# Block 3's output projection as seven quarter-block products, with the steps of blocks 3 to 5 in a new order

## The chip, the core and the metric

The kernel runs on one core of a Trainium2 chip (trn2). The metric is the device time of one execution in microseconds (us). Beside the times of several executions there is one profiled execution, from which all rows shown here come. Engines are named as the profile names them: PE is TensorE, PEld its weight loads, DVE VectorE, ACT ScalarE, POOL GpSimd, SP SyncE, which issues most DMAs.

## What is computed

The inputs q, k, v and alpha have the shape (4, 8, 768, 48): batch B, heads H, positions S, head width D. The first part is a gated linear attention, the second a bilinear feed-forward layer on its 3072 tokens of width 384:

```python
state = np.zeros((B, H, D, D))
for t in range(S):
    state = alpha[:, :, t, :, None] * state + np.einsum('bhd,bhe->bhde', k[:, :, t], v[:, :, t])
    y[:, :, t] = np.einsum('bhd,bhde->bhe', q[:, :, t], state)
x = y.transpose(0, 2, 1, 3).reshape(B * S, H * D)
out = ((x @ w_a) * (x @ w_b)) @ w_out      # 384 -> 1536 -> 384
```

## The kernel before, in words

The work is cut into six blocks (`chunks`, 0 to 5) of 512 tokens: a third of the sequence for two of the four batches. Blocks 4 and 5 are the last third. Each block goes through the attention of its tokens, the two input projections `x @ w_a` and `x @ w_b` in twelve slices f of 128 columns of the hidden width 1536, their product, and the output projection.

The order is written out by hand. `PROGRAM` (L17 on) is a list of steps `block: name arguments; ...`, and the loop at the end of the kernel issues one after the other. Each engine runs its own instructions strictly in that order; between engines, an instruction starts when its inputs are there and when the last readers of what it overwrites are through. PSUM is one tile of eight banks, and the steps name the bank that they use (a step of two banks names the first). The steps that matter here, by engine:

- PE: `a f * i` and `b f * i` (`ff`, L881) are the input projections of slice f into bank i, three matmuls of 512 columns. `o m half i` (`ff_o`, L903) is half of the output projection of 128 tokens, six matmuls of 384 columns. `P n i` and `P+ n i` (`block_mm`, L989) are the products of the other way to project, twelve matmuls of 192 columns each; `P+` adds to what its bank holds. The attention's steps are `K` (L752, state update from keys and values), `D u h i` (L797, scores, two banks), `SB`, `SA` and `Y` (L826, outputs, two banks). u is the batch of the block, h a half of the heads.
- ACT: `as f` (L887) copies an `a` slice out of PSUM into one of three `as_` tiles; `Mc` (L810) copies scores; `vs ... S` copies swapped values; `Tr ... S` copies turned keys (L918); `ot m S` and `z ... S` copy results into staging tiles `ot` (L918).
- DVE: `pr f` (L895) multiplies the two slices into `prod`, of which there are two buffers; `mk` and `mq` (L636) scale keys and queries; `M` (L806) and `Mm` (L814) apply the mask; `k` (L782, L783) updates the state; `X` copies the attention's output to `xT` (ACT L862, DVE L864); `TW n` and `S n` (L960, L971, L974) make the sums that the quarter-block products need; `ot m V` (L920) and `z ... V` (L1001) put results into staging tiles, the latter with an addition.
- SP: `T u` turns keys and queries by a transposing DMA (L705), `dl` loads decays (`bl`, L647), `st` (L936) and `zs` (L1007) store staging tiles.

The quarter-block way splits a block's `prod` (hidden width in two halves kk, tokens in two halves u) and `w_out` (hidden width in two halves, output width in two halves) into quarters and forms the four result quarters c11, c12, c21, c22 from seven products instead of eight:

- Four sums of weights (`TW 1` to `TW 4`), made once, and four sums of `prod` for each block (`S 1` to `S 4`; `S 3` in place of a quarter of `prod`).
- Products 1 and 2 give c11. Products 1 and 6 together are u2; u2 with 5 and 3 is c12; u2 with 7 and 5 is c22; u2 with 7 and 4 is c21. So 1, 6, 7 and 4 follow on each other in one bank, 5 and 3 in another.
- `z p1`, `z u2` and `z p5` copy partial results into staging tiles, `z c11`, `z c12` and `z c22` add one to a product, `z c21` copies.

Before, blocks 4 and 5 go this way and blocks 0 to 3 go through `ff_o`. The fourteen products of blocks 4 and 5 stand one behind the other at the end. A product's result has two groups g of 128 tokens, side by side in one bank. Staging tiles share four buffers. The sums of weights and of `prod` lie in tiles that loads and logarithms of the attention used (`late`, and `la`, of which there is one).

Of the kernel before, what the change touches and what calls it, by code (L numbers as in the profile page):

```python
# [17 lines left out]
0: cm 0; c1; cz 0 b P; ci; ld a 0b Y; c1a; ld a 0a Y; ln 0b; cu; cz 1 b P; fill 7 0; cu2 V; cz 0 q V; cus; ld k 0b Y; ld k 0a Y; B 0b 2; ld q 0b Y  # L18
0: ln 0a; B 0a 0; ld v 0 P; ld q 0a Y; ld a 1 P; cs 0 m P; E 0b i; mk 0b V; ld k 1 P; ld q 1 P; cm 1; W b 0 256; cz 0 v P; E 0b b; mq 0b V; ld v 1 P; W a 256 768; dk 0 2
0: C 0 1 3; E 0a i; mk 0a V; cz 1 q P; E 0a b; mq 0a V; v 0 S; Ce 0 1 V; fill 2 0; W a 0 256; de 0; W b 256 512; C 0 0 1; Ce 0 0 V; D 0 1 2; K 0 0 0; vs 0 0 S; W b 512 768  # L20
0: cs 1 m P
# [78 lines left out]
1: pr 2 0; a 10 0 4; as 10 0; a 7 0 5; M 1 0; a 1 0 6; Mm 1 1 V; b 4 0 7; pr 4 0; b 1 0 1; a 5 0 4; as 1 0; pr 1 0  # L100
# [9 lines left out]
1: as 6 0; a 0 0 0; b 0 0 7; pr 6 0; a 11 0 4; X 1 S; a 2 1 5; b 3 0 2; as 0 0; pr 0 0; as 11 0; a 3 0 3; as 3 0; a 8 0 4; b 9 0 0; b 2 1 1; a 6 1 3; pr 11 0  # L110
1: as 2 1; a 9 0 5; as 9 0; pr 3 0; o 2 0 2
# [252 lines left out]
def kernel(  # L364
# [768 lines left out]
```

## Time and profile before

| what | value |
|---|---|
| times of three runs | 190.29, 189.83, 189.74 us |
| median | 189.83 us |
| profiled execution, own time | 189.66 us |
| its span, first to last instruction | 187.9 us |
| instructions in the span | 6287 |
| granted TensorE clock | full in all slices |

A row of grouped instructions gives the line, the engine, the operation, what it writes and reads with its shapes, the count, then busy time in us and the mean duration of one in ns, and behind the second bar the time that the engine sat idle before them and what released it. A row of the timeline begins with the start in us from the span's start and the time to the end of the group; brackets hold the idle time before it. Matmuls overlap in the pipeline, so their spacing is read from starts and not from durations. A row for a stretch gives its length and then, for PE, PEld, DVE, ACT and POOL, the busy us and the count, then the granted clock, the share of the DMA engines and GB/s.

### The profile page before, as it was taken

The page shows a single profiled execution, that of the slowest core. Times are in us where ns is not written, and L with a number is a line of the kernel's source. Part 1 is how long each engine was busy: PE and PEld are TensorE (multiplying, and loading weights), DVE is VectorE, ACT ScalarE, POOL GpSimd, SP SyncE. Part 2 cuts the span into 40 slices and gives each one's busy share as a digit, 9 for nine tenths or more (in the row PEclk, how much of TensorE's full clock was granted, in tenths as well). Part 3 has the DMA queues.
Part 4 walks back from the last instruction along what each step waited for, and adds up shares of the span by engine and source line. Part 5 has one row for each costly group of instructions (what it writes and reads, how often), then busy time and mean ns, then how long its engine had stood idle before and what let it go on. Part 6 is the DMA issues. An engine that isn't in the chain of part 4 may idle for free.

```text
span 187.9 us, 6287 instructions
## 1 busy us (share of the span) xinstructions
PE 180.7 (96%) x2658; PEld 118.0 (63%) x2673; DVE 149.1 (79%) x267; ACT 119.2 (63%) x225; POOL 51.7 (28%) x74
## 2 busy tenths in 40 slices
PE   7979999999999999999999999999999999999992
PEld 3868885566788876645456645555556444448992
DVE  2587988889979799997898999997487988865641
ACT  4467685678984888796898768942567244443230
POOL 8999573995080510007100006000000000000000
PEclk9999999999999999999999999999999999999999
DMA  5999999999998999999999296989322000000233
GB/s 146 254 224 196 265 236 253 233 249 264 243 223 130 160 236 285 278 254 149 186 245 260 48 161 123 85 115 183 59 85 84 9 0 0 0 0 3 85 130 126
DMA packets 65774, 29.43 MB, mean 157 GB/s; under 512 B 55777, under 2 KB 64113, under 8 KB 65745
## 3 DMA queue, kind: packets, MB, share of 16 engines
q1 hardware_dynamic: 46976, 16.34, 40.9%
q0 software_dynamic: 18624, 12.58, 39.4%
q8 instruction: 21, 0.34, 0.7%
q10 hardware_dynamic: 144, 0.10, 0.2%
q14 instruction: 9, 0.07, 0.1%
HBM read 25.98 MB, written 4.74 MB: 164 GB/s over the span
## 4 chain that ended last, share of the span: by engine, by line
PE 86%; ACT 6%; DMA 3%; issue 2%; POOL 1%; DVE 0%; POOLq 0%
PE psum L881 47%; PE psum L903 16%; PE psum L989 7%; PE psum L826 5%; DMA v_t<-in_v_dram 3%; PE psum L797 3%; ACT vx L918 2%; PE psum L696 2%; PE psum L591 1%; ACT la L514 1%; PE psum L752 1%; PE psum L765 1%; PE psum L658 1%; PE psum L549 1%; PE psum L550 1%
## 5 line engine op out<-in xcount | busy, mean ns | idle before, releaser
L881 PE MATMUL psum<-xT,wa_t 128*128 128x512 bf16 (+1 forms) x264 | 56.5, 336 | 0.5 <-issue 0.2
L881 PE MATMUL psum<-xT,wb_t 128*128 128x512 bf16 (+1 forms) x262 | 56.0, 335 | 0.6 <-issue 0.3
L881 PEld LDWEIGHTS <-wa_t 128*128 128x128 bf16 x270 | 25.8, 98 | 19.9 <-issue 0.5
L881 PEld LDWEIGHTS <-wb_t 128*128 128x128 bf16 x270 | 25.6, 98 | 19.5 <-issue 0.3
L903 PE MATMUL psum<-wo_t,prod 128*128 128x384 bf16 x192 | 34.7, 326 | 0.0
L903 PEld LDWEIGHTS <-prod 128*128 128x128 bf16 x192 | 17.9, 98 | 11.8
L610 POOL TENSOR_TENSOR q_t<-q_t,ra 128x384 f32<-128x384 f32 x6 | 6.1, 1009 | 53.9 <-ACT ra L603 30.9
L918 ACT ACTIVATE ot<-psum 128x384 f32<-128x384 f32 (+1 forms) x20 | 9.7, 485 | 12.1 <-PE psum L989 8.0
L918 ACT ACTIVATE vx<-v_t 32x384 bf16<-32x384 bf16 x26 | 13.5, 521 | 0.5
L810 ACT ACTIVATE m<-psum 128x768 bf16<-128x768 f32 x14 | 11.0, 810 | 3.9 <-PE psum L797 3.9
L636 DVE TENSOR_TENSOR QKp<-q_t,beta 128x768 bf16<-128x768 f32 x10 | 9.5, 954 | 2.8 <-POOL q_t L610 1.7
L514 ACT ACTIVATE la<-a_t 128x1536 f32<-128x1536 f32 (+2 forms) x9 | 9.5, 1055 | 2.9 <-DMA a_t<-in_alpha_dram 2.9
L806 DVE TENSOR_TENSOR m<-psum,mask 128x768 bf16<-128x768 f32 x10 | 9.5, 953 | 0.8 <-PE psum L797 0.6
L636 DVE TENSOR_TENSOR QKp<-k_t,invb 128x768 bf16<-128x768 f32 x10 | 9.5, 954 | 0.3
L826 PE MATMUL psum<-m,vx 64*64 64x128 bf16 (+1 forms) x576 | 8.7, 205 | 0.0
L507 POOL DMA_DIRECT2D v_t<-in_v_dram x8 | 8.5, 1064 | 0.0
L989 PEld LDWEIGHTS <-prod 128*128 128x128 bf16 x96 | 8.0, 98 | 0.2
L1001 DVE TENSOR_TENSOR ot<-psum,ot 128x384 f32<-128x384 f32 x6 | 3.3, 557 | 5.9 <-PE psum L989 5.6
L826 PEld LDWEIGHTS <-vx 64*64 64x64 bf16 x576 | 7.6, 108 | 0.2
L826 PE MATMUL psum<-kqT,Sm 64*64 64x128 bf16 x144 | 7.3, 220 | 0.4 <-DVE Sm L779 0.4
L814 DVE TENSOR_TENSOR m<-m,mask 128x768 bf16<-128x768 bf16 x14 | 7.5, 551 | 0.0
L625 ACT ACTIVATE beta<-psum 128x384 f32<-128x384 f32 x10 | 4.8, 495 | 3.5 <-PE psum L596 3.4
(292 smaller groups left out, 341.2 us busy)
## 6 DMA issues: line engine op xcount, KB each, us to landing
out_dram<-ot SPq DMA_DIRECT2D x23, 192.0 KB, 2.1
q_t<-in_q_dram SPq DMA_DIRECT2D x3, 768.0 KB
k_t<-in_k_dram SPq DMA_DIRECT2D x3, 768.0 KB
a_t<-in_alpha_dram POOLq DMA_DIRECT2D x2, 768.0 KB, 12.1
v_t<-in_v_dram POOLq DMA_DIRECT2D x4, 384.0 KB, 7.5
a_t<-in_alpha_dram SPq DMA_DIRECT2D x2, 768.0 KB
a_t<-in_alpha_dram POOLq DMA_DIRECT2D x3, 384.0 KB, 8.2
k_t<-in_k_dram POOLq DMA_DIRECT2D x3, 384.0 KB, 7.1
```

The source lines that it names most:

```text
L507: eng.dma_start(out=t[:, us, hs].rearrange("p b h r d -> p (b h) (r d)"), in_=src[ch.b0 + us.start:ch.b0 + us.stop, hs, ch.s * 2 * C:(ch.s ...
L514: nc.scalar.activation(out=ch.la[:, us, hs].rearrange("p b h r d -> p (b h r d)"), in_=ch.a[:, us, hs].rearrange("p b h r d -> p (b h r d) ...
L610: eng.tensor_mul(x, x, by)
L636: eng.tensor_mul(QKp[ch.c % 2][:, u, j, :, hs, :D], src[:, u, hs].rearrange("p h r d -> p r h d"), f)
L806: nc.vector.tensor_mul(m, x, maskn())
L810: nc.scalar.activation(out=m, in_=x, func=AF.Copy)
L814: eng.tensor_mul(m, m, maskn())
L826: nc.tensor.matmul(o, lhsT=lhsT, rhs=rhs, start=(g, c) not in begun, stop=False, skip_group_check=True)
L881: nc.tensor.matmul(p, lhsT=(wa_t, wb_t)[w][:, kk, f * 128:(f + 1) * 128], rhs=ch.xT[:, kk, us, :], start=(kk == 0), stop=(kk == KT - 1))
L903: nc.tensor.matmul(op, lhsT=ch.prod[:, f, at:at + C], rhs=wo_t[:, f, :], start=(f == 0), stop=(f == NFF - 1))
L918: nc.scalar.activation(out=o_, in_=i_, func=AF.Copy)
L989: nc.tensor.matmul(o[:, g], lhsT=A[:, f, g * C:(g + 1) * C], rhs=W[:, f], start=(not more and g == 0 and f == 0), stop=(f == LH - 1), skip ...
```

## The change

The matmuls and vector instructions of blocks 0 to 2, and all steps up to block 4's last score step, stay as they are (some long lines of `PROGRAM` are only broken in two). From there on:

- Block 3 is projected by the seven products in place of `o`: four `S`, seven products, seven `z`, and four `zs` for four `st`.
- The steps of blocks 3, 4 and 5 stand in another order and partly in other banks. The products of blocks 3 and 4 now stand between input projections of the next blocks. Block 5's products stand partly between block 4's.
- Block 5's products 1, 6, 7 and 4 use two banks, one for each group g (`Q`, `Q+`: `apart=True`), and the halves of `z c21` are issued in the other order: ACT takes half 1, DVE half 0.
- Staging tiles share six buffers. The tiles for the sums are taken one at a time, when their first sum is made.

The list of steps after, from the point of difference on (the list before stands in the kernel):

```diff
+4: D 1 0 2; Mc 1 0; Y 0
+2: st 3 Y
+5: T 0
+3: b 0 * 4; a 10 * 5
+5: K * 0 2
+4: Mm 1 0 V
+3: as 10 *
+4: SA 1; Y 1; X 1 S
+3: b 10 * 3
+4: X 0 V
+3: pr 0 *; b 7 * 5
+4: a 3 * 7
+5: v 1 V
+4: a 8 * 6; a 6 * 4
+5: vs 1 0 S; T 1; dl
+3: pr 7 *
+4: as 8 *; as 3 *; b 8 * 5; b 3 * 1
+3: pr 10 *
+2: st 0 Y
+4: a 0 * 0
+5: Tr 0 V
+4: as 6 *
+4: pr 8 *; b 0 * 3; pr 3 *
+5: k * 0 V; D 0 0 4; Tr 1 S; D 1 0 6; D 1 1 1
+4: as 0 *; pr 0 *
+5: M 1 0; Mc 0 0
+4: a 9 * 0; b 6 * 5; pr 6 *
+5: Mc 1 1
+4: as 9 *
+5: SB 1 3; vs 1 1 S; D 0 1 1; M 0 1; SB 0 6; Mm 1 1 V; Mm 0 0 V
+4: a 4 * 0; a 11 * 5; as 11 *; TW 1 V; a 7 * 1; as 7 *; b 11 * 2
+5: vs 0 0 V
+4: pr 11 *; b 7 * 5
+3: S 1 V
+5: SA 0
+4: pr 7 *
+5: SA 1; vs 0 1 S; Y 1; Y 0
+3: P 2 1
+5: X 0 V
+4: b 5 * 2
+5: X 1 V
+4: TW 2 V; a 5 * 5
+3: P 1 6
+4: TW 3 V; b 9 * 4; pr 9 *; TW 4 V; a 10 * 3
+3: z p1 1 S
+4: b 2 * 7; as 10 *
+3: z c11 2 V
+4: a 2 * 4
+5: a 4 * 3
+4: as 5 *; pr 5 *
+5: a 0 * 1
+3: S 2 V
+4: as 2 *; pr 2 *; b 10 * 2
+3: S 3 V
+4: pr 10 *; a 1 * 4
+3: P+ 6 6
+4: as 1 *
+3: P 5 5
+5: a 1 * 2
+3: S 4 V
+4: b 4 * 4
+3: z p5 5 S
+4: as 4 *
+5: b 4 * 7
+3: zs c11 Y; P+ 3 5
+5: as 4 *
+3: z u2 6 S; z c12 3 V; P+ 7 6; z c22 7 V
+4: b 1 * 0
+5: a 7 * 3; a 10 * 5
+4: pr 1 *
+5: b 0 * 0; as 0 *
+4: pr 4 *
+3: P+ 4 6
+5: pr 4 *; a 8 * 1; as 8 *; pr 0 *; b 1 * 4; b 7 * 7; b 8 * 0; pr 8 *
+3: zs c22 Y
+5: b 9 * 1
+3: zs c12 Y
+5: as 7 *
+4: P 2 3
+3: z c21 4 S
+5: a 6 * 0; as 1 *; pr 1 *; as 10 *
+4: S 1 V; S 2 V; P 1 6
+5: b 10 * 2; a 5 * 4
+4: z p1 1 S
+5: pr 7 *; as 6 *
+4: P+ 6 6; z c11 2 V
+5: b 6 * 7; a 2 * 0
+4: S 3 V
+5: pr 10 *; pr 6 *
+5: a 9 * 5; b 2 * 7; a 11 * 2; as 2 *; as 9 *; pr 2 *
+4: z u2 6 S
+5: a 3 * 0; as 3 *; b 3 * 3; pr 3 *; b 5 * 5
+4: P 5 0
+5: pr 9 *; b 11 * 3; as 5 *; pr 5 *
+4: P+ 7 6
+5: as 11 *; Q 1 1
+4: z p5 5 S
+5: pr 11 *
+3: zs c21 Y
+5: P 2 7; S 1 V; S 2 V
+4: z c22 7 V; P+ 3 0; z c12 3 V; zs c11 Y; zs c22 Y
+5: S 3 V
+4: P+ 4 6
+5: z p1 1 S
+4: z c21 4 S
+5: S 4 V; Q+ 6 1; z c11 2 V; P 5 0; z u2 6 S
+4: zs c12 Y
+5: Q+ 7 1
+4: zs c21 Y
+5: z p5 5 S; P+ 3 0; z c22 7 V; Q+ 4 1; z c12 3 V; zs c11 Y; zs c22 Y; z c21 4 S 1; zs c12 Y; z c21 4 V 0; zs c21 S 1; zs c21 Y 0
```

The functions:

```diff
@@ -920,12 +960,12 @@
             eng.tensor_copy(o_, i_)
 
     def ff_out(ch, m, eng):
-        ch.ot[m] = wk.tile([128, d_model], F32, name="ot", bufs=4)
+        ch.ot[m] = wk.tile([128, d_model], F32, name="ot", bufs=6)
         evict(ch.ot[m], ch.pf["o", m], eng)
 
     def ff_outc(ch, m, h, eng):
         if m not in ch.ot:
-            ch.ot[m] = wk.tile([128, d_model], F32, name="ot", bufs=4)
+            ch.ot[m] = wk.tile([128, d_model], F32, name="ot", bufs=6)
         evict(ch.ot[m][:, part(h)], ch.pf["oc", m, h], eng)
 
     def rows_of(ch, m):
@@ -953,9 +993,10 @@
         return wo_t[:, kk * LH:(kk + 1) * LH, nn * HM:(nn + 1) * HM]
 
     def mix_w(n, eng):
-        if n == 1:
-            x, y = (late(t)[:, :2 * LH * HM].rearrange("p (w f e) -> p w f e", w=2, f=LH) for t in "ak")
-            mix.update({1: x[:, 0], 2: x[:, 1], 3: y[:, 0], 4: y[:, 1]})
+        at = (n - 1) // 2
+        if 2 * at + 1 not in mix:
+            x = late("ak"[at])[:, :2 * LH * HM].rearrange("p (w f e) -> p w f e", w=2, f=LH)
+            mix.update({2 * at + 1: x[:, 0], 2 * at + 2: x[:, 1]})
         a, b = {1: (quarter(0, 1), quarter(0, 0)), 2: (quarter(1, 1), mix.get(1)), 3: (quarter(1, 1), quarter(0, 1)), 4: (quarter(1, 0), mix.get(2))}[n]
         eng.tensor_sub(mix[n], a, b)
 
@@ -964,8 +1005,10 @@
         p11, p12, p21, p22 = (P[:, kk * LH:(kk + 1) * LH, u * NT // 2:(u + 1) * NT // 2] for u in range(2) for kk in range(2))
         if n == 1:
             x = late("q").rearrange("p (w f e) -> p w f e", w=2, f=LH)
-            y = wk.tile([C, 2, H, 2, D], F32, name="la", bufs=1).rearrange("p b h r d -> p (b h r d)").bitcast(BF16)
-            ch.S = {1: x[:, 0], 2: x[:, 1], 3: p21, 4: y[:, :LH * NT // 2].rearrange("p (f e) -> p f e", f=LH)}
+            ch.S = {1: x[:, 0], 2: x[:, 1], 3: p21}
+        if n == 4:
+            x = wk.tile([C, 2, H, 2, D], F32, name="la", bufs=1).rearrange("p b h r d -> p (b h r d)").bitcast(BF16)
+            ch.S[4] = x[:, :LH * NT // 2].rearrange("p (f e) -> p f e", f=LH)
         S = ch.S
         if n == 1:
             eng.tensor_add(S[1], p21, p22)
@@ -973,7 +1016,7 @@
             a, b = {2: (S[1], p11), 3: (p11, p21), 4: (p12, S[2])}[n]
             eng.tensor_sub(S[n], a, b)
 
-    def block_mm(ch, n, i, more):
+    def block_mm(ch, n, i, more, apart=False):
         P = ch.prod
         pure = {1: (0, 0), 2: (1, 0), 4: (1, 1)}
         if n in pure:
@@ -982,17 +1025,17 @@
         else:
             A = ch.S[{3: 4, 5: 1, 6: 2, 7: 3}[n]]
         W = {1: quarter(0, 0), 2: quarter(1, 0), 3: quarter(1, 1), 4: mix.get(4), 5: mix.get(1), 6: mix.get(2), 7: mix.get(3)}[n]
-        o = bank(i)[:, :2 * HM].rearrange("p (g e) -> p g e", g=2)
+        o = wide(i)[:, :, :HM] if apart else bank(i)[:, :2 * HM].rearrange("p (g e) -> p g e", g=2)
         ch.pf["z", n] = o
         for g in range(2):
             for f in range(LH):
-                nc.tensor.matmul(o[:, g], lhsT=A[:, f, g * C:(g + 1) * C], rhs=W[:, f], start=(not more and g == 0 and f == 0), stop=(f == LH - 1), skip_group_check=True)
+                nc.tensor.matmul(o[:, g], lhsT=A[:, f, g * C:(g + 1) * C], rhs=W[:, f], start=(not more and (apart or g == 0) and f == 0), stop=(f == LH - 1), skip_group_check=True)
 
     def block_out(ch, what, n, eng, half=None):
         hs = slice(0, 2) if half is None else slice(int(half), int(half) + 1)
         x = ch.pf["z", n][:, hs]
         if what not in ch.ot:
-            ch.ot[what] = wk.tile([128, d_model], F32, name="ot", bufs=4).rearrange("p (g e) -> p g e", g=2)
+            ch.ot[what] = wk.tile([128, d_model], F32, name="ot", bufs=6).rearrange("p (g e) -> p g e", g=2)
         o_ = ch.ot[what][:, hs]
         by = {"c11": "p1", "c12": "u2", "c22": "p5"}.get(what)
         if by is None:
@@ -1088,6 +1131,8 @@
         "S": lambda x, n, e: mix_p(x, int(n), ENG[e]),
         "P": lambda x, n, i: block_mm(x, int(n), i, False),
         "P+": lambda x, n, i: block_mm(x, int(n), i, True),
+        "Q": lambda x, n, i: block_mm(x, int(n), i, False, True),
+        "Q+": lambda x, n, i: block_mm(x, int(n), i, True, True),
         "z": lambda x, what, n, e, h=None: block_out(x, what, int(n), ENG[e], h),
         "zs": lambda x, what, e, h=None: block_store(x, what, ENG[e], h),
         "oc": lambda x, m, h, f, i: ff_oc(x, int(m), int(h), int(f), i),
```

More of the change, by code (lines that the diff above doesn't have):

```diff
@@ L17 @@
 PROGRAM = """
[L18 to L21, printed above, removed]
+0: cm 0; c1; cz 0 b P; ci; ld a 0b Y; c1a; ld a 0a Y; ln 0b; cu; cz 1 b P; fill 7 0; cu2 V
+0: cz 0 q V; cus; ld k 0b Y; ld k 0a Y; B 0b 2; ld q 0b Y; ln 0a; B 0a 0; ld v 0 P; ld q 0a Y; ld a 1 P; cs 0 m P
+0: E 0b i; mk 0b V; ld k 1 P; ld q 1 P; cm 1; W b 0 256; cz 0 v P; E 0b b; mq 0b V; ld v 1 P; W a 256 768; dk 0 2
+0: C 0 1 3; E 0a i; mk 0a V; cz 1 q P; E 0a b; mq 0a V; v 0 S; Ce 0 1 V; fill 2 0; W a 0 256; de 0; W b 256 512
+0: C 0 0 1; Ce 0 0 V; D 0 1 2; K 0 0 0; vs 0 0 S; W b 512 768; cs 1 m P
 1: ld a 0 P
```

93 lines of the change are left out of this document (11 added, 82 removed).

## The prediction

> **What bounds the kernel now.** I read the page first: the busy shares, the forty slices, the chain that ended last.
>
> ```profile
> PE 180.7 (96%) x2658; PEld 118.0 (63%) x2673; DVE 149.1 (79%) x267; ACT 119.2 (63%) x225; POOL 51.7 (28%) x74
> PE   7979999999999999999999999999999999999992
> PEclk9999999999999999999999999999999999999999
> PE 86%; ACT 6%; DMA 3%; issue 2%; POOL 1%; DVE 0%; POOLq 0%
> ```
>
> TensorE is busy in every slice and at full clock, and 86% of the chain is its work. The change touches only the stretch from about 124 us on, so the busy time by stretch and the chain's end come next.
>
> ```profile
> 124.44:145.25 20.81, 20.49 (x391) 12.08 (x389) 15.12 (x27) 11.03 (x19) 0.00 (x0) 1.00 0.53 93
> 145.25:170.45 25.20, 24.93 (x116) 11.40 (x118) 20.80 (x30) 10.60 (x18) 0.00 (x0) 1.00 0.02 8
> 170.45:184.31 13.86, 13.86 (x169) 13.79 (x167) 7.46 (x11) 3.59 (x8) 0.00 (x0) 1.00 0.23 78
> ```
>
> The columns after the length are PE, PEld, DVE and ACT busy. PE fills 59.28 of 59.87 us. VectorE has 16.5 us to spare, but it is the second engine (20.80 of 25.20 us in the middle stretch). So what leaves PE leaves the time, provided VectorE and ScalarE still hand over in time; and what follows PE's last instruction counts in full.
>
> **The seven products.** PE in order of time:
>
> ```profile
> 124.44 1.47 PE L881 MATMUL psum<-xT,wb_t 128*128 128x512 bf16 x5
> 125.75 0.81 PE L881 MATMUL psum<-xT,wa_t 128*128 128x512 bf16 x3
> 126.49 0.62 PE L752 MATMUL psum<-v_t,QKp 64*64 64x48 bf16 x28
> 132.03 3.09 PE L903 MATMUL psum<-wo_t,prod 128*128 128x384 bf16 x18
> 134.95 0.81 PE L881 MATMUL psum<-xT,wa_t 128*128 128x512 bf16 x3
> 135.60 0.81 PE L881 MATMUL psum<-xT,wb_t 128*128 128x512 bf16 x3
> 170.45 2.14 PE L989 MATMUL psum<-wo_t,prod 128*128 128x192 bf16 x24
> 183.32 1.15 PE L989 MATMUL psum<-k_t,prod 128*128 128x192 bf16 x12
> 170.61 13.87 PE psum L989 x168
> ```
>
> Durations overlap; starts give the spacing. Eighteen matmuls of 384 columns take 134.95 − 132.03 = 2.92 us, 162 ns each. Thirteen products of twelve 192-column matmuls lie between 170.45 and 183.32: 0.99 us a product, 82.5 ns a matmul. A 512-column step of three takes 0.65 us. Block 3 loses 48 matmuls of 384 columns (48 x 162 = 7.79 us) and gains 7 x 12 of 192 (84 x 82.5 = 6.93 us): **0.86 us less PE**. Nothing else on PE changes in number; the rest is order. A change of shape costs nothing visible (the rows at 134.95 and 135.60 follow on without a gap), so I put 0 for products that now stand singly, at most 0.05 us in all.
>
> A rule of the Trainium skill speaks against this step: "TensorE: Matmul & The Clock Gate", section "Back-to-back issue gap", gives pairs of weight load and matmul a sustained spacing of about 81 ns at 128 columns and 131 ns at 512. By it block 3 would cost at least 84 x 81 = 6.8 us against at most 48 x 131 = 6.3 us, an estimate of 0.5 us lost instead of 0.86 won. The rows disagree: 162 ns at 384 columns.
>
> **What the products add elsewhere.** Grouped by line and shape:
>
> ```profile
> L974 DVE TENSOR_TENSOR la<-prod,q_t 128x1536 bf16<-128x1536 bf16 x2 | 1.9, 950 | 0.0
> L1001 DVE TENSOR_TENSOR ot<-psum,ot 128x384 f32<-128x384 f32 x6 | 3.3, 557 | 5.9 <-PE psum L989 5.6 <-issue 0.3
> L920 DVE COPY ot<-psum 128x384 f32<-128x384 f32 x3 | 1.7, 556 | 0.7 <-PE psum L903 0.7
> L918 ACT ACTIVATE ot<-psum 128x384 f32<-128x384 f32 x9 | 4.4, 491 | 8.0 <-PE psum L989 5.6 <-DVE ot L1001 2.5
> 150.30 0.72 DVE L895 TENSOR_TENSOR prod<-as__3226,psum 128x512 bf16<-128x512 bf16 x1
> 150.58 0.60 ACT L887 ACTIVATE as__3236<-psum 128x512 bf16<-128x512 f32 x1 [0.70 <-PE psum L881]
> ```
>
> VectorE gets four sums (4 x 0.95) and three output adds (3 x 0.56) and loses three copies (3 x 0.56): +3.8 us. ScalarE gets four copies and loses one: +1.5 us. SP still issues four stores for block 3; POOL gets nothing. VectorE then has about 47 of 59 us, so by totals all of it lies beside PE, and only local waits can cost. I laid the new order out by hand with these rows, each step behind its own queue, its inputs, the last reader of its bank and tile. The places that matter:
>
> ```profile
> 125.12 0.95 DVE L636 TENSOR_TENSOR QKp<-k_t,invb 128x768 bf16<-128x768 f32 x1
> 125.99 0.55 DVE L814 TENSOR_TENSOR m<-m,mask 128x768 bf16<-128x768 bf16 x1
> 127.08 0.93 DVE L636 TENSOR_TENSOR QKp<-q_t,beta 128x768 bf16<-128x768 f32 x1
> 123.86 6.12 SPq L705 DMA_TRANSPOSE kqT<-QKp  x2
> 130.08 1.57 SPq L647 DMA_DIRECT2D bl<-row  x2
> 132.55 1.06 ACT L918 ACTIVATE kp<-kqT 128x1024 bf16<-128x1024 bf16 x1
> 133.69 0.56 DVE L783 TENSOR_TENSOR Sm<-tmp,bl 128x384 bf16<-128x384 f32 x1 [0.22 <-DMA bl<-row]
> DMA to landing us min/median/max: 4.7/5.6/6.4
> ```
>
> - `5: K * 0` now stands one 0.65 us step earlier, at 125.84 instead of 126.49. Its second half needs block 5's key product (125.12 + 0.95 = 126.07), its first half (0.3 us) does not. Waiting there costs 0 to 0.23 us; I take **0.1**.
> - `5: mq 1` moves from 127.08 to 126.45, so the second transpose (`T 1`, behind `T 0` on SP) can start at 127.45 instead of about 128.1, and `dl` behind it 0.6 us earlier too. The copy of the turned keys comes at 131.7 on ScalarE, the scores `D 1 0` at 133.55 on PE. In the old run the copy at 132.55 waited for nothing, so that transpose had landed within 4.45 us: at 131.9 here. Margin 0.8 us.
> - `bl` lands by 133.1 to 133.7, the state is ready by 134.2, `SB 1 3` reads it at 135.45.
> - `5: pr 4` is a new wait: `prod` has two buffers, so it stands on VectorE until block 3's last product `P+ 4` is through (159.05), with `pr 0` and `pr 8` queued behind it. It ends at 160.0; PE wants its bank (7) for `b 7` at 160.35.
> - The sums share single tiles with the next block (`la`), and each new user comes over 10 us after the last reader; six staging tiles do the same for the stores (the closest is `5: z p5`, 1.5 us behind a landing).
> - The closest handovers: `a 7 * 1` behind `M 0 1` (0.2 us), `a 2 * 4` behind `pr 9`, `b 0 * 0` behind `pr 1`, `b 8 * 0` behind `pr 0`, `b 2 * 7` behind `pr 6` (0.35 each), `a 4 * 0` and `D 0 1 1` (0.4).
>
> No other step of PE waits in this layout.
>
> **The last sum in two banks.**
>
> ```profile
> 183.52 0.56 DVE L1001 TENSOR_TENSOR ot<-psum,ot 128x384 f32<-128x384 f32 x1 [0.38 <-PE psum L989]
> 184.51 0.33 ACT L918 ACTIVATE ot<-psum 128x192 f32<-128x192 f32 x1 [2.43 <-PE psum L989]
> 184.87 0.37 ACTq L1007 DMA_DIRECT2D out_dram<-ot  x1
> 184.87 0.36 DVE L920 COPY ot<-psum 128x192 f32<-128x192 f32 x1 [0.79 <-ACT ot L918]
> 127.94 0.81 ACT L862 ACTIVATE xT<-psum 128x768 bf16<-128x768 f32 x1 [0.68 <-PE psum L826]
> 127.94 0.94 DVE L864 CAST xT<-psum 128x768 bf16<-128x768 f32 x1
> L1007 SPq DMA_DIRECT2D out_dram<-ot x8: 344/372/383, 173.3 to 185.3; - x8
> DMA to landing us min/median/max: 1.7/1.8/2.0
> ```
>
> PE ends at E = 184.47. ScalarE reads half 0, VectorE's half 1 waits for ScalarE although PE is done, and the last store is issued at 185.25 (E + 0.78). Is it the shared bank or the shared tile? At 127.94 both engines write halves of one tile from different banks at the same moment, so I take the bank. With two banks VectorE reads half 0 while PE still fills the other: `c12` ends at E − 0.39, half 0 at E − 0.10, its store is issued on SP at E + 0.02 behind that of `c12` (0.37). ScalarE takes half 1 from E + 0.04 to E + 0.37 and issues at E + 0.40. Last issue E + 0.40 instead of E + 0.78: **0.38 us less**, with the same 1.7 to 2.0 us of landing behind it.
>
> **Sum.** 189.66 (span 187.9 and 1.76 around it) − 0.86 − 0.38 + 0.1 = 188.52. The median of the runs shown, 189.83, is 0.17 above the profiled execution; carried there the sum is 188.69. I say **188.6**.
>
> **Rivals.** Two more rows bear on them:
>
> ```profile
> L989 PEld LDWEIGHTS <-prod 128*128 128x128 bf16 x96 | 8.0, 98 | 0.2
> 145.41 1.89 PE L881 MATMUL psum<-xT,wb_t 128*128 128x512 bf16 x8 [0.16 <-issue]
> ```
>
> 1. *Tail unchanged.* The wait belonged to the tile `ot`, or half 1's order brings it back: 188.6 + 0.38 = 189.0. For it: the profile names `ot`. Against: the two writers at 127.94. Chance 0.08.
> 2. *VectorE's handovers become the bound.* Some eight places have margins of 0.2 to 0.45 us, and four sums of 0.95 us stand in front of products that free banks. Where lateness beyond the margin is 0.1 us a place the time is 188.6 + 0.8 = 189.4 (chance 0.12); at 0.25 a place it is 190.6, slower than before (0.08). It decides from 0.15 a place, where the 1.2 us are gone. Against: VectorE idles before most products in the old order.
> 3. *Late keys.* `T 1` takes the longest landing seen, 6.4 us: 133.85, copy until 134.9, `D 1 0` 1.4 us late: 190.0. Stalls start from a landing at 132.5. For: the spread 4.7 to 6.4; against: this very transpose took at most 4.45. Chance 0.05.
> 4. *Weight loads set the pace* of products that stand singly, 98 ns (the loads' mean) in place of 82.5: 12 x 15.5 = 0.19 us a product, 21 products 3.9 us, 192.5, and the change no longer does what it says; slower from seven products on. Against: 168 in a row ran at 82.5 with the same loads. Chance 0.03. The page's rule above points this way.
>
> 5. *Better than the sum*, 188.2: idle stretches like the 0.16 us here do not come back and `K` does not wait. Chance 0.06.
>
> **Numbers.** The forecast has 0.58. A change of 0.3%, 0.57 us, is about what this measurement can tell from none: faster means below 189.26. Faster holds the forecast, rivals 1 and 5 and a quarter of 2's milder case, 0.75; same the rest of it and rival 3, 0.14; slower 0.11. The range 188.1 to 189.8 leaves out rivals 3, 4 and the hard case of 2 (0.16) and little below; the forecast's own is 188.2 to 189.0.
>
> **What would show it.** Right: 84 more matmuls of 192 columns and no L903 matmul in the last 60 us; PE spacing 0.99 us a product wherever it stands; PE's last matmul 0.7 to 0.9 us earlier; VectorE's last copy before ScalarE's, not behind it; the last store 0.4 us behind PE's end. Wrong: PE idle ahead of L797 or L826 near 133 (keys), PE idle ahead of L881 put down to VectorE between 136 and 170 (handovers), or products spaced at 1.1 us and more.

## The result and the profile after

| kernel | median | lowest to highest | runs |
|---|---|---|---|
| before | 190.22 us | 189.49 to 193.12 | 22 |
| after | 189.42 us | 188.45 to 191.23 | 22 |

The ratio of after to before is 0.9954, 95% interval 0.9932 to 0.9975: 0.46%, about 0.87 us, faster, and most of the interval lies beyond the 0.3% that counts as a change. The forecast was 188.6 us in a range of 188.1 to 189.8. Of the 0.8 us between forecast and median, 0.4 belongs to the kernel before: its 22 runs have a median of 190.22 us, the three shown earlier had 189.83. The line that the prediction drew for "faster", 189.26, lay 0.3% below those three; the median of 189.42 misses it, but it is below 189.65, which is 0.3% under 190.22.

The profiled execution of the kernel after took 190.44 us, which is longer than that of before (189.66). Its page shows why that is no contradiction:

```profile
PE 181.9 (96%) x2693; PEld 122.3 (65%) x2709; DVE 152.6 (81%) x271; ACT 120.1 (64%) x228; POOL 53.6 (28%) x74
PEclk9987999999999999999999999999999999999999
```

In the third and fourth of the forty slices the granted clock is 8 and 7 tenths instead of full. That is the first part of the program, which the change leaves alone, and it came out 1.83 us longer in this execution: block 4's output step `Y 0`, the last one before the orders differ, starts at 125.64 us instead of 123.81. The same first part scatters by over 2 us among the fourteen profiles of this study (123.52 to 126.09). So I measure from there: **the stretch** runs from the start of block 4's `Y 0` to the end of the span. It falls into **PE's part**, up to the start of the last product, and the rest, which holds that product's 1.15 us and **the tail** behind it. The stretches of the kernel before and of the kernel after (length, then busy us of PE, PEld, DVE, ACT and POOL, the granted clock, DMA share, GB/s):

```profile
123.81:183.32 59.51, 58.93 (x719) 36.91 (x716) 43.45 (x67) 25.84 (x45) 0.00 (x0) 1.00 0.25 55
183.32:187.89 4.57, 1.15 (x14) 0.92 (x12) 0.92 (x2) 0.33 (x1) 0.00 (x0) 1.00 0.38 129
```

```profile
125.64:184.30 58.66, 58.13 (x752) 39.14 (x751) 46.48 (x71) 26.35 (x48) 0.00 (x0) 1.00 0.25 57
184.30:188.66 4.36, 1.16 (x15) 0.93 (x12) 0.85 (x2) 0.33 (x1) 0.00 (x0) 1.00 0.41 137
```

At full clock throughout, the stretch went from 59.51 + 4.57 = 64.08 us to 58.66 + 4.36 = 63.02: PE's part lost 0.85 us and the tail 0.21 (4.57 − 1.15 = 3.42 to 3.21). The page has just the four instructions more on VectorE and three more on ScalarE that were counted. Added one by one, their durations behind `Y 0` are 3.8 and 1.5 us more, as was costed; the busy time in the rows above rose by only 3.0 and 0.5, because records of neighbouring instructions overlap. In order of time, the kernel after:

```profile
127.67 0.65 PE L792 MATMUL psum<-v_t,QKp 64*64 64x48 bf16 x28
129.29 1.86 SPq L745 DMA_TRANSPOSE kqT<-QKp  x1
133.81 1.06 ACT L958 ACTIVATE kp<-kqT 128x1024 bf16<-128x1024 bf16 x1
134.94 0.72 PE L837 MATMUL psum<-kqT,kp 64*64 64x128 bf16 x48
144.77 1.15 PE L1032 MATMUL psum<-wo_t,prod 128*128 128x192 bf16 x12
145.76 0.81 PE L921 MATMUL psum<-xT,wb_t 128*128 128x512 bf16 x3
160.63 0.73 DVE L935 TENSOR_TENSOR prod<-as__3290,psum 128x512 bf16<-128x512 bf16 x1 [1.59 <-PE psum L1032]
```

PE's whole list of waits from 125.64 us on has one line, the 0.16 us of issue that it also had before. Such a list can miss a short wait (one of 0.22 us follows below that no list shows), so the length of PE's part is the stronger evidence.

`K` starts 2.03 us after `Y 0`, which is exactly the step's place in the forecast's layout without its wait of 0.1. A product that stands singly takes 0.99 us (144.77 to 145.76), as the fourteen in a row did. The expected wait of `5: pr 4` is there, on VectorE, and costs PE nothing. The end of the kernel after:

```profile
182.62 0.49 ACT L958 ACTIVATE ot<-psum 128x384 f32<-128x384 f32 x1 [0.59 <-DMA out_dram<-ot]
184.30 1.15 PE L1032 MATMUL psum<-k_t,prod 128*128 128x192 bf16 x12
185.00 0.36 DVE L960 COPY ot<-psum 128x192 f32<-128x192 f32 x1
185.49 0.33 ACT L958 ACTIVATE ot<-psum 128x192 f32<-128x192 f32 x1 [2.38 <-PE psum L1032]
185.85 0.37 ACTq L1050 DMA_DIRECT2D out_dram<-ot  x1
```

VectorE's copy now stands before ScalarE's and has no wait, and the last store is issued at E + 0.40 (E, PE's last end, is 184.30 + 1.15 = 185.45). The last issue is the forecast to the hundredth, yet the tail gained 0.21 us and not 0.38. The first row is unforeseen: the copy `5: z p5` waits 0.59 us for a store to leave its staging tile.

### The profile page after: what moved, and what is told of

It is laid out like the page before. It is cut to its first block, busy times and chain, and to the rows that moved or that the text cites. A ratio compares the mean times of both kernels' runs of the same rounds, so it can differ in the third digit from the quotient of the medians.

```text
span 188.7 us, 6347 instructions
## 1 busy us (share of the span) xinstructions
PE 181.9 (96%) x2693; PEld 122.3 (65%) x2709; DVE 152.6 (81%) x271; ACT 120.1 (64%) x228; POOL 53.6 (28%) x74
## 4 chain that ended last, share of the span: by engine, by line
PE 90%; ACT 6%; issue 2%; DVE 1%
PE psum L921 47%; PE psum L943 12%; PE psum L1032 11%; PE psum L866 5%; PE psum L837 3%; PE psum L589 2%; PE psum L590 2%; PE psum L736 2%; PE psum L572 2%; ACT vx L958 2%; PE psum L631 1%; ACT la L554 1%; PE psum L792 1%; PE psum L805 1%; PE psum L698 1%
## 5 line engine op out<-in xcount | busy, mean ns | idle before, releaser
L921 PE MATMUL psum<-xT,wa_t 128*128 128x512 bf16 (+1 forms) x262 | 55.2, 335 | 0.5 <-issue 0.2
L943 PE MATMUL psum<-wo_t,prod 128*128 128x384 bf16 x144 | 26.1, 327 | 0.0
L958 ACT ACTIVATE ot<-psum 128x384 f32<-128x384 f32 (+1 forms) x23 | 11.2, 487 | 17.7 <-PE psum L1032 15.4
L943 PEld LDWEIGHTS <-prod 128*128 128x128 bf16 x144 | 13.3, 98 | 8.3
L1032 PEld LDWEIGHTS <-prod 128*128 128x128 bf16 x144 | 12.0, 98 | 1.2
L676 DVE TENSOR_TENSOR QKp<-k_t,invb 128x768 bf16<-128x768 f32 x10 | 10.1, 1013 | 0.3
L1044 DVE TENSOR_TENSOR ot<-psum,ot 128x384 f32<-128x384 f32 x9 | 5.0, 555 | 5.9 <-issue 3.2
L665 ACT ACTIVATE prod<-psum 128x384 f32<-128x384 f32 x8 | 3.5, 488 | 6.0 <-PE psum L590 6.0
```

What stands on the lines that cost most here:

```text
L676: eng.tensor_mul(QKp[ch.c % 2][:, u, j, :, hs, :D], src[:, u, hs].rearrange("p h r d -> p r h d"), f)
L921: nc.tensor.matmul(p, lhsT=(wa_t, wb_t)[w][:, kk, f * 128:(f + 1) * 128], rhs=ch.xT[:, kk, us, :], start=(kk == 0), stop=(kk == KT - 1))
L943: nc.tensor.matmul(op, lhsT=ch.prod[:, f, at:at + C], rhs=wo_t[:, f, :], start=(f == 0), stop=(f == NFF - 1))
L958: nc.scalar.activation(out=o_, in_=i_, func=AF.Copy)
L1032: nc.tensor.matmul(o[:, g], lhsT=A[:, f, g * C:(g + 1) * C], rhs=W[:, f], start=(not more and (apart or g == 0) and f == 0), stop=(f == LH ...
```

## The experiments

**The theory**: PE is full in the stretch, so the time falls by what PE no longer does (0.86 us) and by what two banks save at the end; the new order only makes this possible. **The rivals**: the order itself is worth something, with or without the products; the end's gain comes from the tile's or the queue's order and not from the bank; the thin margins (keys, sums, staging tiles) already cost part of the gain. The numbers of all profiles:

| kernel | PE's part | tail | stretch | median | ratio to before, 95% |
|---|---|---|---|---|---|
| before | 59.51 | 3.42 | 64.08 | 190.22 | |
| after | 58.66 | 3.21 | 63.02 | 189.42 | 0.9954 [0.9932, 0.9975] |
| new_again | 58.88 | 3.21 | 63.24 | 189.05 | 0.9942 [0.9917, 0.9967] |
| new_third | 58.66 | 3.20 | 63.01 | 189.42 | 0.9956 [0.9930, 0.9983] |
| old_products_new_order | 59.54 | 3.20 | 63.89 | 189.86 | 1.0000 [0.9985, 1.0015] |
| new_products_old_places | 65.21 | 3.42 | 69.78 | 195.79 | 1.0312 [1.0284, 1.0340] |
| two_banks_old_order | 59.51 | 3.20 | 63.86 | 190.00 | 0.9987 [0.9955, 1.0019] |
| one_bank_end | 58.66 | 5.02 | 64.83 | 191.19 | 1.0040 [1.0013, 1.0068] |
| one_bank_sp_stores | 58.85 | 3.97 | 63.97 | 190.15 | 1.0013 [0.9988, 1.0038] |
| late_keys | 62.91 | 3.23 | 67.29 | 193.60 | one run |
| extra_sum | 58.91 | 3.22 | 63.28 | 188.68 | one run |
| four_tiles | 61.86 | 3.04 | 66.76 | 191.42 | 1.0056 [1.0023, 1.0090] |
| p5_apart | 58.66 | 3.32 | 63.14 | 189.29 | 0.9948 [0.9922, 0.9974] |
| p5_apart_split | 58.67 | 3.18 | 63.00 | 189.03 | 0.9928 [0.9896, 0.9961] |

The lengths come from one profile each. Each ratio is to runs of the kernel before that were taken beside it, whose median lay between 189.91 and 190.22 us. The runs of one kernel scatter by up to 3.6 us, much of it from the unchanged first part, so differences below 0.5 us are read from the stretch alone.

**The kernel after, unaltered, twice more** (`new_again`, `new_third`).

> The changed kernel unaltered. Measure, here and below: the stretch from block 4's first output step (Y 0) to the end of the span (64.08 us before, 63.05 after in the two profiles) and PE's part of it, from Y 0 to the start of the last product (59.51 and 58.66). Theory: the stretch is set by PE and repeats to 0.1 us, 63.05 and 58.66, while the time of the whole kernel scatters by a microsecond because of the unchanged first 120 us. Rival: the stretch scatters as much as the whole time, and the gain of 1.03 us in it is chance.

> The changed kernel unaltered, a third profile beside the next three. Of the two so far one has PE's part at 58.66 and one at 58.88, with a wait of PE ahead of block 5's product 3, whose bank the copy p5 had not yet read because its staging tile waited for a store. Theory: how late that store lands differs from run to run, so PE's part is anything from 58.66 to 58.9. Rival: one of the two was an accident of other origin, and the wait for the store is not what PE feels.

Both repeat the gain. In `new_again` PE's part is 0.22 us longer, and its rows at the end show why:

```profile
181.00 1.15 PE L1032 MATMUL psum<-k_t,prod 128*128 128x192 bf16 x12
181.67 0.49 ACT L958 ACTIVATE ot<-psum 128x384 f32<-128x384 f32 x1 [0.97 <-DMA out_dram<-ot]
182.22 1.15 PE L1032 MATMUL psum<-wo_t,la 128*128 128x192 bf16 x12
```

`5: P+ 3` adds into the bank that `5: z p5` reads. The copy waits 0.97 us for the store here, ends at 182.16 us, and the product starts 1.22 us after the one ahead of it instead of 0.99. So such a wait is free up to about 0.75 us here (an estimate, 0.97 − 0.22). In the kernel after (0.59) and in `new_third` it costs nothing, here 0.22 us.

**Products without the order, order without the products.** `old_products_new_order` puts block 3's `o`, `ot` and `st` back into the new order (`S`, `z`, `zs` go):

```diff
-3: S 1 V
-3: P 2 1
+3: o 2 0 1
-3: P 1 6
+3: o 2 1 -
-3: z p1 1 S
+3: ot 2 S
...
-3: P+ 6 6
+3: o 1 0 6; o 1 1 -
```

> The changed kernel's order with block 3 projected as before: eight halves of six 384-column matmuls where the seven products stand, four copies and four stores, none of block 3's four sums. Theory: PE is packed in both, so PE's part grows by what the products save, 0.86 us, to 59.5, and the stretch from 63.05 to 63.9. Rival: the gain comes from the order (fewer idle gaps on PE), and the products are worth little: PE's part stays near 58.7.

`new_products_old_places` puts the products and sums into the order of before, where `o`, `ot` and `st` stood, with six staging tiles and the old end:

```diff
-3: o 2 0 2; b 10 * 5
+3: P 1 7; b 10 * 5
-3: pr 10 *; pr 7 *
+3: pr 10 *; pr 7 *; z p1 1 S; S 1 V
+4: TW 1 V; TW 2 V
+3: S 2 V
-3: o 2 1 -
+3: P 2 6; z c11 2 V; zs c11 Y
-3: o 1 0 0; o 1 1 -
+3: P+ 6 7; P 5 5
...
```

> The kernel before with block 3's seven products put where its eight halves stood, its sums and the sums of weights ahead of them, six staging tiles, nothing else moved, the end in one bank. Theory: in that stretch (20.8 us) VectorE had 15.1 us of work and gets 6.4 more, so it becomes the bound, products wait for sums and PE stands idle: PE's part 1 to 3 us longer than 59.51 and the kernel slower than before. Rival: the products alone carry the gain and the new order is worth nothing: PE's part 58.66.

The first has PE's part at 59.54 us, 0.03 from before: **the order by itself is worth nothing**, and the products are worth 59.54 − 58.66 = 0.88 us, where 0.86 was forecast. (Its ratio is 1.0000 although it has the new end; the interval, 0.29 us to either side, is too wide to show that 0.2.) The second lost 5.7 us. Its list of PE's waits (in total, times, longest):

```profile
PE psum L990 <- DVE q_t L975: 1.3, 1, 1.3
PE psum L990 <- DVE prod L975: 1.2, 1, 1.2
PE psum L990 <- ACT xT L860: 0.9, 1, 0.9
...
PE psum L795 <- ACT as__3007 L885: 0.7, 1, 0.7
```

Six waits of 0.7 to 1.3 us make 5.7 (the two left out are 0.8 each, for VectorE's mask at L804 and its output add at L1002). Against a PE that loses nothing, 59.51 − 0.86 = 58.65 us, the loss is 6.6, so about 0.9 us lies in delays that the list doesn't show. I had expected 1 to 3 us. The largest two waits are for the sums (L975), which are on the path when a product stands right behind its last `pr`. The order earns nothing by itself, but in the old places the 0.88 us could not be had.

**The last sum: bank, tile or queue.** `two_banks_old_order` makes only the edit of the end in the kernel before:

```diff
-5: P 1 1; z p1 1 S; P 2 2; ... P+ 6 1; ... P+ 7 1; ... P+ 4 1; z c21 4 S 0; z c21 4 V 1; zs c21 S 0; zs c21 Y 1
+5: Q 1 1; z p1 1 S; P 2 4; ... Q+ 6 1; ... Q+ 7 1; ... Q+ 4 1; z c21 4 S 1; z c21 4 V 0; zs c21 S 1; zs c21 Y 0
```

> The kernel before with only the last chain of products in two banks and the halves in the new order. PE's part stays 59.51. Theory of the prediction: stretch 63.70 (0.38 us less); second theory (stores without a gap): 63.88; rival: no change, 64.08.

`one_bank_end` undoes that edit in the kernel after (`P` for `Q`, and `z c21 4 S 0; z c21 4 V 1; zs c21 S 0; zs c21 Y 1`):

> The changed kernel with block 5's chain of products back in one bank and the halves of the last copy in the old order. Theory of the prediction: the shared bank makes the two copies follow on each other and the last store is issued 0.38 us later, all of which reaches the end: stretch 63.43. Second theory: the last 394 KB of stores keep the DMA engines busy without a gap behind PE's end, so that only about 0.2 us of it counts: 63.25. Rival: the wait belongs to the staging tile and is there with two banks as well: 63.05. PE's part stays 58.66 in all.

`one_bank_sp_stores` is `one_bank_end` with both halves stored from SP (`zs c21 Y 0; zs c21 Y 1`):

> The kernel one_bank_end with both halves of the last result stored by SP, none by ScalarE. There the store that ScalarE issued took 2.30 us to issue instead of 0.37 and its bytes left last; nobody had expected that. Theory: only that issue was held up, and without it the end comes about 0.3 to 0.4 us later than with two banks (the two copies behind each other and two issues behind each other on one queue): stretch 63.35 to 63.5. Rival: the hold-up belongs to the last store, whoever issues it, and the stretch stays near 64.8.

The edit alone leaves PE's part at 59.51 us and shortens the tail from 3.42 to 3.20. With one bank, `one_bank_end` (rows below) and `one_bank_sp_stores` (0.80 us) show VectorE waiting for ScalarE, one and the same wait as before, in a kernel whose tile is no other than in the kernel after:

```profile
184.78 2.30 ACTq L1050 DMA_DIRECT2D out_dram<-ot  x1
184.78 0.36 DVE L960 COPY ot<-psum 128x192 f32<-128x192 f32 x1 [0.79 <-ACT ot L958]
```

So it is the **bank**: the two halves still share the tile `ot` in the kernel after, ScalarE's copy is still issued first there, and the wait is gone. The edit also swaps the halves between the two engines; what the swap alone is worth was not run. The Trainium skill says in "PSUM — Partial Sum Buffer", section "PSUM bank collisions raise a hardware error", that a compiler's scheduler puts a dependency between instructions of two engines on the same bank and the same 32 partitions, reads included; these rows agree, with 0.79 us of it.

Why 0.21 us and not 0.38? The windows of the kernel after and then of before, behind PE's end:

```profile
185.50:186.00 0.50, 0.00 (x0) 0.00 (x0) 0.00 (x0) 0.33 (x1) 0.00 (x0) 1.00 0.36 125
186.00:186.25 0.25, 0.00 (x0) 0.00 (x0) 0.00 (x0) 0.00 (x0) 0.00 (x0) 1.00 0.90 301
...
187.00:187.25 0.25, 0.00 (x0) 0.00 (x0) 0.00 (x0) 0.00 (x0) 0.00 (x0) 1.00 0.94 316
187.25:187.50 0.25, 0.00 (x0) 0.00 (x0) 0.00 (x0) 0.00 (x0) 0.00 (x0) 1.00 0.06 15
```

```profile
185.50:185.75 0.25, 0.00 (x0) 0.00 (x0) 0.00 (x0) 0.00 (x0) 0.00 (x0) 1.00 0.56 169
...
186.25:186.50 0.25, 0.00 (x0) 0.00 (x0) 0.00 (x0) 0.00 (x0) 0.00 (x0) 1.00 0.76 249
186.50:186.75 0.25, 0.00 (x0) 0.00 (x0) 0.00 (x0) 0.00 (x0) 0.00 (x0) 1.00 0.02 3
```

(Last column: GB/s.) Before, the last stores' data left room (169 and 249 GB/s) and ended at about 186.5, 2.03 us after PE's end of 184.47. After, it runs at 301 to 329 GB/s without a gap from 186.0 to 187.25, which is 1.80 behind PE's end. The last store is issued 0.38 us earlier relative to PE, but its bytes queue with those of `c12` and of the other half, and arrive only 0.2 us earlier. The packets of ScalarE's queue give the size: in both kernels ScalarE's half is issued at E + 0.40, but its bytes cross from E + 1.28 to E + 1.74 before and from E + 1.43 to E + 1.89 after, because SP's half, issued at E + 0.79 before, now comes at E + 0.10. These 0.15 us are nearly all that is missing from the 0.38.

`four_tiles` (below) is the counter-check. There a slow clock sets the last stores apart: `c12` is issued at E − 1.02, SP's half at E − 0.26 and ScalarE's at E + 0.40 as always. PE ends at 187.23, and the engines are free when ScalarE's bytes come, from E + 1.27 to E + 1.71:

```profile
188.23:188.48 0.25, 0.00 (x0) 0.00 (x0) 0.00 (x0) 0.00 (x0) 0.00 (x0) 1.00 0.02 3
188.48:188.73 0.25, 0.00 (x0) 0.00 (x0) 0.00 (x0) 0.00 (x0) 0.00 (x0) 1.00 0.72 249
```

Its tail is 3.04 us, 0.38 shorter than before's: where the bytes don't meet, the whole forecast gain is there.

The tail of `one_bank_end`, 5.02 us, was expected by neither theory: ScalarE's store takes 2.30 us to issue there where the same issue takes 0.37 in the kernel before, all of its 12 runs lie between 190.68 and 191.56 us, and the last bytes cross after 187.5 us. What makes this issue slow stays open. In the middle of it the trace has a transfer of 8 KB of the kind that the page calls instruction (185.57 to 185.92 us); in the kernel before the last such transfer crosses at 182.54, ahead of the issue, and in the kernel after at 187.21, behind it. Whether the issue waited for it is not shown. With SP issuing that store the stretch is 63.97 us, above the 63.35 to 63.5 of its theory and below its rival's 64.8. The tail is 3.97, 0.55 longer than the kernel before's, which also has one bank, and 0.45 of that is the last sixteenth of the last store: fifteen of its sixteen landings come 1.69 us after its issue (184.71), the sixteenth after 2.14, again with an 8 KB instruction transfer beside it (185.31 to 185.96). More on such late landings stands in the last section.

**The keys** (`late_keys`): `5: mq 1` and `T 1; dl` stand later, behind three more VectorE steps. (The list of steps ahead of the prediction does not show three steps that stand in both kernels: `5: mq 1 V` behind `4: SA 1; Y 1; X 1 S`, `5: v 0 V` ahead of `4: pr 8 *`, and `4: S 4 V` behind `5: pr 10 *; pr 6 *`.)

```diff
-5: mq 1 V
...
-5: vs 1 0 S; T 1; dl
+5: vs 1 0 S
 3: pr 7 *
+5: mq 1 V; T 1; dl
```

> The changed kernel with block 5's second query product, and the transpose and loads behind it, moved back behind three vector steps (about 2.1 us later). Theory: the keys had 0.8 us to spare in the changed kernel, so about 1.3 us of PE idle time appear ahead of the scores and PE's part grows by 1.0 to 1.6 us. Rival: the margin is larger than 2 us and nothing moves.

```profile
131.04 1.84 SPq L745 DMA_TRANSPOSE kqT<-QKp  x1
135.77 1.06 ACT L958 ACTIVATE kp<-kqT 128x1024 bf16<-128x1024 bf16 x1 [3.43 <-DMA kqT<-QKp]
136.88 0.86 PE L837 MATMUL psum<-kqT,kp 64*64 64x128 bf16 x32 [2.68 <-ACT kp L958]
```

```profile
136.00:137.00 1.00, 0.12 (x7) 0.12 (x11) 0.00 (x0) 1.00 (x2) 0.00 (x0) 0.73 0.43 137
...
139.00:140.00 1.00, 1.00 (x4) 0.23 (x2) 0.38 (x1) 0.75 (x2) 0.00 (x0) 0.57 0.00 0
```

The transpose is issued 131.04 − 124.54 = 6.50 us after `Y 0` instead of 129.29 − 125.64 = 3.65, 2.85 us later (in the kernel before it was 4.27), and its landing takes 4.73 us. PE's part grew by 4.25 us where 1.0 to 1.6 were expected: 2.68 of idle PE, and a granted clock (third column from the end) of 0.5 from 136.46 to 139.86 us (a mean of 0.73 over 136 to 137 means 0.54 us of it at half clock, and so on), in which work takes twice as long. PE's work from 136.88 to 139.86 at half clock costs 1.5 us beside the 2.68, which together is nearly all of the 4.25. The mechanism of the rival on late keys is shown, at about three times its price; it is one profile of one run. In the kernel after the copy starts at most 4.52 us behind the issue and ends at 134.87; the second of the three score steps of the row at 134.94, which needs it, starts at 135.14. So the margin is under 0.3 us, not 0.8.

**VectorE's margins** (`extra_sum`): `3: S 2 V` is made twice, 0.95 us more of VectorE (the sum is the same).

> The changed kernel with block 3's second sum made twice (0.86 us more VectorE in front of the handovers of the next seven steps). Theory of the prediction: margins and the idle stretch of VectorE behind them take it up, PE's part grows by 0 to 0.2 us. Rival 2 of the prediction (VectorE's handovers bind): PE's part grows by 0.5 to 0.86 us.

```profile
147.01 1.93 DVE L1017 TENSOR_TENSOR q_t<-q_t,prod 128x1536 bf16<-128x1536 bf16 x2
149.00 1.93 PEld L1032 LDWEIGHTS <-q_t 128*128 128x128 bf16 x24 [0.43 <-DVE q_t L1017]
151.12 0.81 PE L921 MATMUL psum<-xT,wa_t 128*128 128x512 bf16 x2
```

Products 6 and 5 wait for the doubled sum and take 2.12 us instead of 1.98; with 0.11 at their start that is the 0.25 us by which PE's part is longer (58.91). The other 0.70 us of the sum were absorbed at this place, and nothing behind it came later. The 0.25 is a little above the 0 to 0.2 of the theory and well below the 0.5 to 0.86 of rival 2: here the handovers do not add up their lateness, and PE's part of 58.66 us leaves no room for lateness in the kernel after. It is one profile, and one place was tried. Another place is thin too: in `one_bank_sp_stores`, where only the end differs, VectorE idles 0.44 us ahead of its state step (L823), most likely for the decays `bl`, and PE's part is 0.19 us longer.

**The staging tiles.** `four_tiles` is the kernel after with `bufs=4` for `ot`.

> The changed kernel with four staging tiles in place of six. Theory: with four, block 5's u2 copy has to wait until the store of block 4's c12 has landed (issued about when that copy could start, 2.1 us to landing), and product 7, which adds to the bank that this copy reads, waits on PE: PE's part 0.8 to 1.1 us longer, 59.5 to 59.8, the stretch about 64, most of the gain gone. Rival: the stores land in time and the number of tiles is worth nothing: 58.66 and 63.05.

```profile
181.26 0.56 DVE L1044 TENSOR_TENSOR ot<-psum,ot 128x384 f32<-128x384 f32 x1 [1.53 <-DMA out_dram<-ot]
...
182.45 1.22 PE L1032 MATMUL psum<-k_t,prod 128*128 128x192 bf16 x12 [2.08 <-ACT ot L958]
183.46 2.13 PE L1032 MATMUL psum<-wo_t,la 128*128 128x192 bf16 x12
185.38 1.85 PE L1032 MATMUL psum<-k_t,prod 128*128 128x192 bf16 x12
```

VectorE's addition waits for a store, behind it stand ScalarE's copies, and behind those a product: 2.08 us of idle PE. Then a product takes 185.38 − 183.46 = 1.92 us instead of 0.99, since the granted clock fell again:

```profile
183.00:183.50 0.50, 0.50 (x9) 0.50 (x7) 0.00 (x0) 0.00 (x0) 0.00 (x0) 0.90 0.73 235
183.50:186.50 3.00, 3.00 (x21) 2.85 (x19) 1.12 (x2) 0.00 (x0) 0.00 (x0) 0.50 0.21 68
186.50:187.00 0.50, 0.50 (x7) 0.48 (x4) 0.36 (x1) 0.00 (x0) 0.00 (x0) 0.69 0.01 2
```

PE's part is 3.20 us longer, 0.8 to 1.1 was expected, and the whole is slower than before: **six tiles are part of the gain**. The median of its 12 runs is 2.0 us above the kernel after's, so this profile's price is higher than that of most runs. The wait at 181.26 hangs on one late landing: of the store that it waits for (issued at 176.77), fifteen landings come within 1.97 us and the sixteenth after 4.40. VectorE was idle from 179.73 on, so with the fifteen alone it would not have waited. `p5_apart` goes the other way and gives `z p5` a tile that the attention no longer uses:

```diff
-            ch.ot[what] = wk.tile([128, d_model], F32, name="ot", bufs=6).rearrange("p (g e) -> p g e", g=2)
+            x_ = wk.tile([C, 2, P2, D], F32, name="tmp").rearrange("p b a d -> p (b a d)") if what == "p5" else wk.tile([128, d_model], F32, name="ot", bufs=6)
+            ch.ot[what] = x_.rearrange("p (g e) -> p g e", g=2)
```

> The changed kernel with the staging tile of p5 taken from a pair of tiles that the attention no longer uses, so that no copy near the end waits for a store. Theory: ScalarE's wait for a store goes, PE's part is 58.66 in every run, the stretch 63.05, the median 0.1 us below the changed kernel's. Rival: the wait moves to another tile and PE's part stays between 58.66 and 58.9.

```profile
182.97 0.49 ACT L958 ACTIVATE tmp<-psum 128x384 f32<-128x384 f32 x1 [0.50 <-PE psum L1032]
```

The copy now waits for PE alone and PE's part is 58.66 us, the best value of the others. The stretch is 63.14 us and not 63.05: the last bytes cross by E + 1.89 as in the kernel after, and the 0.1 us lies behind them. `p5_apart_split` adds to it that block 5's products 5 and 3 use two banks and `c12` leaves in halves:

```diff
-5: S 4 V; Q+ 6 1; z c11 2 V; P 5 0; z u2 6 S
+5: S 4 V; Q+ 6 1; z c11 2 V; Q 5 3; z u2 6 S
-... P+ 3 0; ... z c12 3 V; zs c11 Y; zs c22 Y; z c21 4 S 1; zs c12 Y; ...
+... Q+ 3 3; ... z c12 3 V 0; zs c11 Y; zs c22 Y; zs c12 Y 0; z c12 3 V 1; z c21 4 S 1; zs c12 Y 1; ...
```

> As p5_apart, and block 5's products 5 and 3 in two banks too, so that the first half of c12 is read and stored half a product earlier, in two stores. Theory (the last 394 KB go out without a gap and start with c12): the stores start earlier and the end comes 0.1 to 0.15 us sooner, stretch 62.9. Rival: the end hangs on the last half's store alone (0.95 us to its first byte, 0.33 us of bytes, 1.4 us to the end), and nothing or less than 0.05 us is gained; one more issue on SP could even cost 0.1.

The tail is 3.18 us, 0.03 less than in the kernel after, so the theory (0.1 to 0.15) missed and its rival held. `c12` is out earlier and the data now leaves room (190 to 231 GB/s from E + 0.5 to E + 1.25), but ScalarE's half still crosses only from E + 1.37 to E + 1.82, beside SP's half, which is issued at E + 0.17. Its ratio is the lowest of the study, but its interval overlaps that of the kernel after, so a gain over that is not shown.

## Why the prediction held, step by step

- **PE is the bound, so what leaves PE leaves the time.** Right: PE's part fell by 0.85 us (0.88 less by the products, 0.03 more by the order).
- **The seven products, 0.86 us.** Right, by two rows of before (162 ns and 82.5 ns a matmul). The rule of the Trainium skill that spoke against it, "TensorE: Matmul & The Clock Gate", section "Back-to-back issue gap", would have made the stretch longer by 0.5 us, by the prediction's estimate; the trace does not agree. Rival 4 falls with the 0.99 us of the products that stand singly.
- **`5: K * 0`, 0.1 us lost.** It waited for nothing: 0.1 too much.
- **VectorE and ScalarE beside PE.** Right for the totals, and for the handovers as far as `extra_sum` tried them; the layout came out as written, with PE's waits at 0.16 us. Rival 2 did not come.
- **The keys, margin 0.8 us.** Right that they don't cost; the margin is under 0.3, since the copy starts 0.3 us later and the score step 0.2 us earlier behind `Y 0` than in the layout, and the price of a stall was 4.25 us for a delay of 2.85. Rival 3 did not come because the landing took at most 4.52 us, less than the least (4.7) of before's row. That is partly luck.
- **Six staging tiles, `5: z p5` 1.5 us behind a landing.** Wrong. It assumed the 2.0 us of before's longest landing. `z p5` takes over block 4's `c22` tile (the sixth allocation back), whose store is issued at 178.88 in the kernel after and lets go at 182.62, 3.7 us later. Fifteen of its sixteen landings come within 1.97 us, and with them alone the copy would not have waited; the sixteenth takes 3.64, beside a 16 KB instruction transfer (179.83 to 181.22). In the repeats it takes 4.02 and 3.64. The wait costs 0 or 0.22 us in the three profiles of the kernel after.
- **The last sum, 0.38 us.** The mechanism was right (the bank, and the issue at E + 0.40), the size was not: 0.21. The failing words are "with the same 1.7 to 2.0 us of landing behind it". That row held for a last store that came alone; the two halves are now issued 0.3 us apart, and ScalarE's bytes cross 0.15 us later behind the same issue.
- **The sum.** −0.86 − 0.38 + 0.1 = −1.14 was forecast; the stretch gave −0.85 − 0.21 = −1.06, and −0.84 and −1.07 in the repeats. That the sum is only 0.08 off is partly luck: the 0.17 that the end did not give is set against the 0.10 that `K` did not cost. The forecast of 188.6 also stands 0.09 under its own sum of 188.69 without a reason. The −0.87 us of the measured ratio is uncertain by 0.4 and holds all of these.

## What to carry to other kernels

When one engine is full, price an exchange of instruction shapes by the spacing of starts in the same trace; that came out within 0.02 us, where the order around it decided between 0.9 us won and 5.7 lost. Time behind the last instruction does not shrink with the last issue alone: look at whether the last bytes already flow without a gap. Where buffers wait for stores, a few landings that came on time are not the longest that can come: look at what else the DMA engines carry at the new place. Measure a small change from the last common instruction on, not over the whole span.

## What the runs showed of the hardware

- An idle PE cost more than its idle time in two runs: around 2.08 us (`four_tiles`) and 2.68 us (`late_keys`) without a matmul the granted clock fell to 0.5 for 3.4 us (183.40 to 186.81, 136.46 to 139.86), which takes up to 1.7 us more (an estimate: half of 3.4). Six waits of up to 1.3 us in `new_products_old_places` left the clock at 1.00. The Trainium skill, "TensorE: Matmul & The Clock Gate", section "What's actually happening", has a free-running window of about 3.4 us that lowers the clock after an idle one. The length agrees; the condition does not, since PE worked for over 1 us in the 3.4 us ahead of both falls.
- A store lets go of its tile with the last of its sixteen landings (182.51 us for the copy at 182.62 in the kernel after), and one of them can come late. Landings of the 192 KB stores that the page's view counts took 1.7 to 2.0 us in the kernel before and 1.8 to 3.8 in `new_third` (least, median, most):

```profile
DMA to landing us min/median/max: 1.8/2.1/3.8
```

The 3.8 belongs to a store that stands alone: it is issued at 161.28 us, its neighbours at 156.55 and 166.06. Fifteen landings come within 1.97 us. The window from 161 to 166 us, in forty slices, shows the last 12 KB trickle behind the rest, and an instruction transfer of 16 KB (162.01 to 163.76) in the same window:

```profile
GB/s 0 0 0 0 0 0 0 0 131 129 295 326 289 320 117 0 0 0 0 0 0 6 6 12 6 12 12 25 18 0 0 0 0 0 0 0 0 0 0 0
q8 instruction: 1, 0.02, 2.2%
```

The store at 166.06 has no such transfer near it, and all sixteen land within 1.98 us. Of 160 stores issued behind 150 us in the fourteen profiles (the slow one of `one_bank_end` is left out), 39 have their last landing more than 0.4 us behind the fifteenth, and each of the 39 has an instruction transfer of 8 or 16 KB under way at some time between 0.5 and 2.3 us behind its issue. Not every such transfer makes a store late, and that the late sixteenth shares a DMA engine with it is read from the times alone. In the kernel before no store behind 150 us was late.

- A store's issue on ScalarE took 2.30 us in `one_bank_end`, against 0.37 in the kernels before and after. Its cause stays open.
